# One tensor for keys and values, swapped slots, and six loads in place of nine for the last values

## The chip, the cores and the metric

The kernel runs on one core of one Trainium2 chip. The metric is the device time of one execution in microseconds (us); lower is better. The kernel before takes 1301.44 us (median of three runs, 1301.37 to 1301.44).

## The reference, cut to what matters

One decode step for two sequences (B = 2), width 448, 16 heads of 256, a cache of 8192 keys and values for each head and sequence, in float32. After the attention comes a gated bilinear feed-forward part of width 1792.

```python
q = (layernorm(x) @ wq)                       # 2 x 1 x 448 -> 16 heads x 256
scores = einsum("bhqd,bhkd->bhqk", q, k_cache) * 256 ** -0.5
p = softmax(scores)
o = einsum("bhqk,bhkd->bhqd", p, v_cache)
h = x + o.reshape(2, 1, 4096) @ wo
n = layernorm(h)
out = h + ((n @ w_gate) * (n @ w_up)) @ w_down
```

There are 32 pairs of head and sequence, called queries 0 to 31 here. Each reads 8 MiB of keys and 8 MiB of values once; with the weights that is 561 MB.

## The kernel before, in words

**Rows and loads.** A query's 8192 keys lie on 128 partitions, 64 keys on each, and one key has 256 floats. So a key tile or a value tile is 64 "rows" of 1 KB in every partition, and one row over all partitions is 128 KB of traffic. `k_sb` has 112 rows: two slots of 64 that share 16 rows (`k_base`, `OVER`). Even queries use rows 0 to 63, odd ones 48 to 111. `v_sb` has 64 rows. Nearly all loads are issued by SyncE (SP) on one queue, in program order; an issue waits until the rows that it overwrites are free, and all issues behind it wait too.

**One query.** VectorE (DVE) multiplies the keys by the query in place (`tensor_mul`) and sums over the 256 floats (`tensor_reduce`), in two parts: first the 16 rows that the next query's slot shares, then the other 48 (`score_parts`). `top` takes the maximum, `softmax` makes the weights p on ScalarE (ACT) with two small products on TensorE (PE), `mix` multiplies p with the values on PE in 64 matmuls of 512 columns, two rows of values for every two of them, and `mixed` turns the result and multiplies it with wo.

**Order of loads.** The loop at line 612 issues, in step n, the values of query n-1, then the keys of query n+1. PE runs the steps of the first `LOOP` queries in a hardware loop (`turns`). For the last queries (`LATE`, lines 25 to 30) the values come in several loads, so that rows freed early are filled early: query 28 in 48 and 16 rows, 29 in 32 and 32, 30 in 32 and 32 (the second into the rows of query 30's own keys), 31 in 16, 32 and 16. With a second part, step n loads the first part, then the keys n+1, then the second part. The keys of queries 30 and 31 (`FINE`) are scored in four parts of 16 rows.

**The end.** After query 31's scores come its softmax and `mix`; `open_sums` copies the residual sum out of PSUM (two DVE copies) and starts two sums with 16 small matmuls; it stands between the second and the third part of query 31's values. Then `last_head` (wo of head 15), the layer norm, `project` with w_gate, `project` twice with w_up, and `down` with w_down, whose tiles arrive in four loads (`DOWN`). The weights of this part are loaded into key rows as they come free. Small tiles of the end live in free value rows (`guest`, `late_guest`).

Of the kernel before, what the change touches and what calls it, by code (L numbers as in the profile page):

```python
# [7 lines left out]
ALU = mybir.AluOpType  # L8
AX = mybir.AxisListType
# [3 lines left out]
P = 128  # L13
# [5 lines left out]
OVER = HC  # L19

AHEAD = 24
FIRST = ((NJ - AHEAD, NJ), (0, NJ - AHEAD))


LATE = (
    ((48, None), (16, None)),
    ((32, None), (32, None)),
    ((32, None), (32, ("k", 0))),
    ((16, ("k", 32)), (32, ("v", 32)), (16, ("v", 0))),
)  # L30
WQ, WO = 3 * 2 * DH + DH, 2 * D
WALL = 2 * WQ + 4 * WO
# [183 lines left out]
def decode_block(nc, x, k_cache, v_cache, w, wg, wu, wd, out):  # L216
# [3 lines left out]
    def sb(name, *shape):  # L220
        return nc.alloc_sbuf_tensor(name, list(shape), F32)[:]
# [20 lines left out]
        put("PE", "transpose", out, in_, ident[:n, :n], r=(*r, "ident"), w=w, mark=mark)  # L242

    sb("align", P, ALIGN)
    k_sb = sb("k_sb", P, 2 * NJ - OVER, DH)
    v_sb = sb("v_sb", P, NJ, DH)
    w_sb = sb("w_sb", P, WALL)
    buffers = {"k": k_sb, "v": v_sb}
    v_flat = v_sb.rearrange("p j d -> p (j d)")

    def guest(name, at, rows, *shape):

        n = 1
        for k in shape:
            n *= k
        o.homes[name] = ("v", at, n)
        got = v_flat[:rows, at : at + n]
        if len(shape) > 1:
            dims = "abc"[: len(shape)]
            got = got.rearrange(f"p ({' '.join(dims)}) -> p {' '.join(dims)}", **dict(zip(dims, shape)))  # L260
        return got
# [5 lines left out]
        h, b = divmod(i, B)  # L267
        return cache[b, h].rearrange("(p j) d -> p j d", p=P)[:, lo:hi, :]

    def load_keys(name, cache, i, lo, hi, buf, at, event=None):  # L270
        o.load(
            "SP", name, buffers[buf][:, at : at + hi - lo, :], keys(cache, i, lo, hi),
            writes=[(buf, at * DH, (at + hi - lo) * DH)], event=event,
        )

    def k_base(i):
        return i % 2 * (NJ - OVER)

    def load_k(i, lo=0, hi=NJ):
        load_keys(f"d_k_{i}_{lo}", k_cache, i, lo, hi, "k", k_base(i) + lo)  # L280

    def v_parts(i):
        got, lo = [], 0
        for n, place in LATE[i - EARLY] if i >= EARLY else ((NJ, None),):
            buf, at = place or ("v", lo)
            got.append((lo, lo + n, buf, at))
            lo += n
        return got

    def load_v(i, part):  # L290
        lo, hi, buf, at = part
        load_keys(f"d_v_{i}_{lo}", v_cache, i, lo, hi, buf, at, "e_v" if i < LOOP else None)

    def load_w(name, k, lo, hi, event=None):
        o.load("SP", name, w_sb[:, lo:hi], w[k][:, lo:hi], writes=[("w", lo, hi)], event=event)
# [5 lines left out]
        return 2 * WQ + h % 4 * WO  # L301

    load_w("d_w0", 0, 0, WQ)
    for lo, hi in FIRST:
        load_k(0, lo, hi)

    ident = sb("ident", P, P)
    put("POOL", "memset", ident, 0.0, w=["ident"])
# [134 lines left out]
    def score_parts(i):  # L443
        if i == 0:
            return list(FIRST)
        at = [(k - 1) % (NJ // HC) * HC if i % 2 == 0 else k * HC for k in range(NJ // HC)]
        if i in FINE:
            return [(lo, lo + HC) for lo in at]
        return [(at[0], at[0] + HC), (at[1], at[1] + NJ - HC)]

    def scores(i, part, between=None):
        h, b = divmod(i, B)
        s, name = s_t[i % 2], f"s{i % 2}"
        lo, hi = score_parts(i)[part]
        at = k_base(i) + lo
        kt = k_sb[:, at : at + hi - lo, :]
        qk, there = kt, ("k", at * DH, (at + hi - lo) * DH)
        if i == 0 and part == 0:
            qk, there = v_sb[:, : hi - lo, :], ("v", 0, (hi - lo) * DH)
        q, slot = qs[b], q_at(h)  # L460
        here = ("k", at * DH, (at + hi - lo) * DH)
        dve(
            "tensor_mul", qk, kt, q[:, slot, :][:, None, :].to_broadcast([P, hi - lo, DH]),
            r=[here, (f"q{b}", slot, slot + 1)], w=[there],
        )
        if between is not None:
            between()
        dve("tensor_reduce", s[:, lo:hi], qk, axis=AX.X, op=ALU.add, r=[there], w=[(name, lo, hi)])

    def top(i):  # L470
        dve("tensor_reduce", m, s_t[i % 2], axis=AX.X, op=ALU.max, r=[f"s{i % 2}"], w=["m"],
# [24 lines left out]
    def mix(i, parts):  # L496
        k = other(i)
        with common(i):
            take("e_v", i, 16)
            for lo, hi, buf, at in parts:  # L500
                for t in range(lo // 2, hi // 2):
                    g, j = 32 * (t % 4), at + 2 * t - lo
                    mm(
                        o_ps[k][g : g + 2, :], p_t[k][:, 2 * t : 2 * t + 2],
                        buffers[buf][:, j : j + 2, :], t < 4, t >= NJ // 2 - 4,
                        r=[f"p{k}", (buf, j * DH, (j + 2) * DH)], w=[f"o_ps{k}"],
                        mark="PE" if t == hi // 2 - 1 else None,
                    )

# [71 lines left out]
    def group(t, q):  # L581
        return t[:, q * YW : (q + 1) * YW]

    late_at = [HC * DH]

    def late_guest(name, rows, *shape):
        got = guest(name, late_at[0], rows, *shape)
        late_at[0] += o.homes[name][2]
        assert late_at[0] <= 2 * HC * DH
        return got  # L590

    h_sb = late_guest("h_sb", B, DC * P)
# [19 lines left out]
    for n in range(NQ + 1):  # L612
        hp, at = divmod(n, 2 * B)
        parts = v_parts(n - 1) if n > 0 else []
        if n > 0:
            load_v(n - 1, parts[0])
        if n < NQ:
            scores(n, 0, (lambda: softmax(n - 1)) if n > 0 else None)
        else:
            softmax(n - 1)  # L620
        if late is not None:
            mix(n - 2, late)
            mixed(n - 2)
            late = None
        if n + 1 < NQ:
            load_k(n + 1)
        for part in parts[1:]:
            load_v(n - 1, part)
        if n % 8 == 1:
            k = n // 8 + 1  # L630
            load_w(f"d_w_{k}", k, WQ if k == H // 4 else 0, WALL, event("e_w", n))
        def norm_last():
            if n > 0:
                norm(n - 1)

        if n == NQ:
            norm_last()
        else:
            for part in range(1, len(score_parts(n))):
                scores(n, part, norm_last if part == 1 else None)  # L640
        if n == NQ:
            mix(n - 1, parts[:-1])
            open_sums()
            mix(n - 1, parts[-1:])
            mixed(n - 1)
        elif n + 1 < NQ and len(parts) > 1:
            late = parts[1:]
            mix(n - 1, parts[:1])
        elif n > 0:
            mix(n - 1, parts)  # L650
            mixed(n - 1)
        if at == 2 and hp + 1 < H // 2:
            queries(n - 1, hp + 1)
        if n < NQ:
            if n == 0:
                o.ops["PE"].append(lambda: turns())
            top(n)

    k_flat = k_sb.rearrange("p j d -> p (j d)")
    places = {"wd": 0, "wg": (NJ - OVER) * DH, "wu": (NJ - OVER) * DH + NF * D}  # L660
    wd_t, wg_t, wu_t = (k_flat[:, places[n] :][:, : NF * D] for n in ("wd", "wg", "wu"))
    for name, t, src in (("wg", wg_t, wg), ("wu", wu_t, wu)):
        for k, half in enumerate(PIECES[name]):
            o.load("SP", f"d_{name}_{k}", t[:, half], src[:, half],
                   writes=[("k", places[name] + half.start, places[name] + half.stop)])
    at = 0
    for n in DOWN:
        o.load("SP", f"d_wd_{at}", wd_t[:, at * D : (at + n) * D], wd[:, at * D : (at + n) * D],
               writes=[("k", at * D, (at + n) * D)])
        at += n  # L670

    o.load(
# [6 lines left out]

    def project(out, out_name, t, name, k, between=None):  # L680
        wide, piece = WIDE[{"wg": "B_w_gate", "wu": "B_w_up"}[name]][k], PIECES[name][k]
        here = ("k", places[name] + piece.start, places[name] + piece.stop)
        t = t[:, piece]
        for c in range(DC):
            for g in range(4):
                xs = xr[:, c]
                if c < DC - 1:
                    at = c * sum(wide) + sum(wide[:g])
                else:
                    xs = xr[:, c + g % 2]  # L690
                    at = 3 * sum(wide) + (wide[0] if g >= 2 else 0)
                mm(
                    out[32 * g : 32 * g + 32, : wide[g]], xs.rearrange("p b r -> p (b r)"),
                    t[:, at : at + wide[g]], c == 0, c == DC - 1, r=["xr", here], w=[out_name],
                    mark="PE" if c == DC - 1 and g == 3 else None,
                )
            if c == 1 and between is not None:
                between()
# [54 lines left out]
    def down(lo, hi):  # L753
        for k in range(lo, hi):
            n, g = FF[k]
            for q in range(YN):
                mm(
                    y_ps[32 * q : 32 * q + 32, :], hmT[n // 2][:, n % 2, g, :],
                    wd_t[:, k * D + q * YW : k * D + (q + 1) * YW], False, k == NF - 1,
                    r=[f"hmT{n // 2}", ("k", k * D, (k + 1) * D)], w=["y_ps"],  # L760
                    mark="PE" if k == NF - 1 and q == YN - 1 else None,
                )

# [94 lines left out]
```

## Time and profile before

| | |
|---|---|
| Median of three runs | 1301.44 us (1301.37 to 1301.44) |
| Profiled execution, span from first to last instruction | 1300.5 us |
| Around the span (median less span) | 0.9 us |
| DMA queue of SyncE, share of 16 engines' span | 99.8% (561.3 MB) |
| DVE busy | 1130.8 us (87%) |
| PE busy | 488.8 us (38%) |
| ACT busy | 62.6 us (5%) |
| TensorE clock granted, mean | 0.654 |

An engine's busy time is a mean over the whole span. Here one query follows the other with the same pattern for some 1150 us, and the last 150 us, in which the loads of the last queries and of the feed-forward weights and the final products run, are another stage with its own limits.

### The profile page before, as it was taken

The numbers are of one execution on the slowest core, as the hardware profiler recorded it, in microseconds if no ns is written. First come the engines' busy times: TensorE is split into PE (matmuls) and PEld (weight loads), VectorE is DVE, ScalarE is ACT, GpSimd is POOL, SyncE is SP. The second block draws the span as 40 slices with busy tenths as digits, with TensorE's granted clock in tenths as the row PEclk, the third lists the DMA queues.
The fourth block names the chain that finished last, engine by engine and source line by source line (L and its number), as shares of the span: only waits on it lengthen the run. The fifth ranks groups of instructions, "written<-read, shape, count | busy, mean of one in ns | idle before, by whom it ended". The sixth has DMA issues, their size and how long they took to land.

```text
span 1300.5 us, 6955 instructions
## 1 busy us (share of the span) xinstructions
PE 488.8 (38%) x2972; PEld 168.9 (13%) x2972; DVE 1130.8 (87%) x275; ACT 62.6 (5%) x184; POOL 1.4 (0%) x9
## 2 busy tenths in 40 slices
PE   3035422363331633215343063432424334243368
PEld 2011100120100201002101021010111001010113
DVE  7996988888988689888889868898888897889991
ACT  1000000000000000000000000000000000000000
POOL 0000000000000000000000000000000000000000
PEclk8566756686656766558666576665766667666578
DMA  9999999999999999999999999999999999999998
GB/s 414 423 434 448 424 437 431 427 441 423 448 424 435 448 423 443 427 439 429 435 435 423 433 448 423 448 424 443 427 443 427 423 436 445 426 438 429 435 433 374
DMA packets 12111, 561.45 MB, mean 432 GB/s; under 512 B 1602, under 2 KB 1732, under 8 KB 1988
## 3 DMA queue, kind: packets, MB, share of 16 engines
q1 hardware_dynamic: 12096, 561.30, 99.8%
q8 instruction: 6, 0.10, 0.0%
q14 instruction: 5, 0.04, 0.0%
q10 hardware_dynamic: 4, 0.00, 0.0%
HBM read 561.19 MB, written 0.11 MB: 432 GB/s over the span
## 4 chain that ended last, share of the span: by engine, by line
DMA 70%; DVE 29%; PE 0%; issue 0%; SPq 0%
DMA k_sb<-in_A_k_cache_dram 68%; DVE k_sb L229 14%; DVE s L229 14%; DMA k_sb<-in_wd_dram 2%; DVE nm L229 0%; PE y_ps L229 0%; SPq L176 0%; DVE m L229 0%; PE sm L229 0%; DVE v_sb L229 0%; DVE rl L229 0%
## 5 line engine op out<-in xcount | busy, mean ns | idle before, releaser
L229 DVE TENSOR_TENSOR k_sb<-k_sb,q 128x12288 f32<-128x12288 f32 (+2 forms) x67 | 549.6, 8203 | 130.3 <-DMA k_sb<-in_A_k_cache_dram 130.3
L229 DVE TENSOR_REDUCE s<-k_sb 128x48 f32<-128x12288 f32 (+2 forms) x67 | 549.3, 8198 | 0.2
L229 PE MATMUL o_ps<-v_sb,p 128*2 128x512 f32 x2000 | 288.2, 739 | 397.7 <-PEq L183 387.6
L229 PEld LDWEIGHTS o_ps<-v_sb,p 128*2 128x2 f32 x2000 | 53.7, 97 | 603.8 <-issue 591.3
L229 PE MATMUL sm<-nm,ones 1*128 1x1 f32 x64 | 16.6, 326 | 191.7 <-PEq L183 175.1
L229 PE MATMUL sm<-ident,m 128*1 128x128 f32 x32 | 10.9, 341 | 137.0 <-PEq L183 106.1
L229 PE MATMUL q_ps<-w_sb,xb 128*128 128x256 f32 (+1 forms) x172 | 59.3, 503 | 0.0
L229 ACT ACTIVATE o_sb<-o_ps 128x512 f32<-128x512 f32 x32 | 19.1, 597 | 703.9 <-PE o_ps L229 703.9
L229 PE MATMUL sm<-sel,o_sb 128*128 128x1 f32 x256 | 33.7, 253 | 25.8 <-PEq L183 22.9
L229 PE MATMUL acc_ps<-w_sb,oT 128*2 128x448 f32 x60 | 36.6, 749 | 15.9 <-PEq L183 11.0
L229 PEld LDWEIGHTS sm<-nm,ones 1*128 1x128 f32 x64 | 14.6, 283 | 201.2 <-issue 183.5
L229 PEld LDWEIGHTS sm<-sel,o_sb 128*128 128x128 f32 x256 | 31.8, 195 | 55.6 <-issue 48.2
L229 PEld LDWEIGHTS q_ps<-w_sb,xb 128*128 128x128 f32 x172 | 33.7, 200 | 30.0 <-issue 27.6
L229 PE MATMUL sm<-lsum,ones 128*128 128x1 f32 x64 | 17.5, 342 | 26.0 <-PEq L183 23.1
L229 ACT ACTIVATE nb<-sm 128x1 f32<-128x1 f32 x32 | 5.5, 171 | 395.7 <-PE sm L229 395.7
L229 PEld LDWEIGHTS sm<-ident,m 128*1 128x1 f32 x32 | 2.6, 81 | 149.8 <-issue 115.3
L229 PEld LDWEIGHTS sm<-lsum,ones 128*128 128x128 f32 x64 | 15.6, 303 | 28.0 <-issue 24.7
L229 ACT ACTIVATE q<-q_ps,rstd 128x512 f32<-128x512 f32 (+1 forms) x18 | 11.5, 640 | 71.9 <-PE q_ps L229 71.9
L229 PE MATMUL o_ps<-k_sb,p 128*2 128x512 f32 x48 | 9.3, 934 | 6.1 <-DMA k_sb<-in_A_v_cache_dram 6.1
L229 ACT ACTIVATE p<-s,nb 128x64 f32<-128x64 f32 x32 | 11.1, 347 | 1.0
L229 DVE TENSOR_TENSOR v_sb<-k_sb,q 128x6144 f32<-128x6144 f32 x1 | 6.6, 6557 | 4.8 <-DMA k_sb<-in_A_k_cache_dram 4.8
L229 PE MATMUL q_ps<-k_sb,xr 128*32 128x256 f32 (+3 forms) x96 | 10.0, 506 | 1.6 <-DMA k_sb<-in_B_w_gate_dram 1.6
(79 smaller groups left out, 85.1 us busy)
## 6 DMA issues: line engine op xcount, KB each, us to landing
v_sb<-in_A_v_cache_dram SPq DMA_DIRECT2D x4, 4096.0 KB, 30.5
w_sb<-in_w_dram SPq DMA_DIRECT2D x3, 3584.0 KB, 37.8
v_sb<-in_A_v_cache_dram SPq DMA_DIRECT2D x1, 6144.0 KB, 24.3
k_sb<-in_A_k_cache_dram SPq DMA_DIRECT2D x1, 5120.0 KB, 24.6
v_sb<-in_A_v_cache_dram SPq DMA_DIRECT2D x2, 2048.0 KB, 27.3
k_sb<-in_A_v_cache_dram SPq DMA_DIRECT2D x1, 4096.0 KB, 35.3
k_sb<-in_B_w_gate_dram SPq DMA_DIRECT2D x1, 3136.0 KB, 32.4
k_sb<-in_A_k_cache_dram SPq DMA_DIRECT2D x1, 3072.0 KB, 11.6
```

The source lines that it names most:

```text
L229: o.put(engine, lambda: f(*args, **kw), r, w, mark, event)
```

## The change

- Keys and values share one tensor `c_sb` of 176 rows: rows 0 to 111 for keys as before, rows 112 (`RING`) to 175 for values. The total size is unchanged.
- The key slots are swapped: even queries use rows 48 to 111, odd ones 0 to 63. The first 24 keys of query 0 go to the value rows and are multiplied in place there; before, 24 keys were loaded to their key rows and their product was written to the value rows.
- `LATE` has three entries, so query 28's values are one load of 64 rows and belong to the hardware loop. Query 29's come in 32 and 32 rows, query 30's in one load of 64 rows to rows 64 to 127 (48 key rows and 16 value rows), query 31's in 44 rows (rows 128 to 171) and 20 rows (rows 64 to 83).
- The product of query 30's first 16 keys is written to rows 160 to 175, not in place.
- `open_sums` stands before all of query 31's `mix`.
- The feed-forward weights' places: w_gate from row 0, w_up from row 24.5, w_down from row 84.

```diff
-FIRST = ((NJ - AHEAD, NJ), (0, NJ - AHEAD))
+FIRST = ((0, AHEAD), (AHEAD, NJ))
+RING = 2 * NJ - OVER
 LATE = (
-    ((48, None), (16, None)),
-    ((32, None), (32, None)),
-    ((32, None), (32, ("k", 0))),
-    ((16, ("k", 32)), (32, ("v", 32)), (16, ("v", 0))),
+    ((32, RING), (32, RING + 32)),
+    ((64, NJ),),
+    ((44, RING + HC), (20, NJ)),
 )
...
     def k_base(i):
-        return i % 2 * (NJ - OVER)
+        return (1 - i % 2) * (NJ - OVER)
...
-        at = [(k - 1) % (NJ // HC) * HC if i % 2 == 0 else k * HC for k in range(NJ // HC)]
+        at = [(k - i % 2) % (NJ // HC) * HC for k in range(NJ // HC)]
...
-        at = k_base(i) + lo
-        kt = k_sb[:, at : at + hi - lo, :]
-        qk, there = kt, ("k", at * DH, (at + hi - lo) * DH)
-        if i == 0 and part == 0:
-            qk, there = v_sb[:, : hi - lo, :], ("v", 0, (hi - lo) * DH)
+        at = RING if i == 0 and part == 0 else k_base(i) + lo
+        to = RING + NJ - HC if i == NQ - 2 and part == 0 else at
+        k_t, t = (c_sb[:, r : r + hi - lo, :] for r in (at, to))
+        here, there = rows(at, hi - lo), rows(to, hi - lo)
...
         if n == NQ:
-            mix(n - 1, parts[:-1])
             open_sums()
-            mix(n - 1, parts[-1:])
+            mix(n - 1, parts)
             mixed(n - 1)
...
-    places = {"wd": 0, "wg": (NJ - OVER) * DH, "wu": (NJ - OVER) * DH + NF * D}
+    places = {"wg": 0, "wu": NF * D, "wd": (NJ + 20) * DH}
```

## Rows read from the trace of the kernel before

**Rows 1.** The page: span, throughput by slice, the load queue's share.
```profile
span 1300.5 us, 6955 instructions
...
GB/s 414 423 434 448 424 437 431 427 441 423 448 424 435 448 423 443 427 439 429 435 435 423 433 448 423 448 424 443 427 443 427 423 436 445 426 438 429 435 433 374
...
q1 hardware_dynamic: 12096, 561.30, 99.8%
```

**Rows 2.** Timeline of DVE: start, duration, tiles; idle before and its releaser.
```profile
1159.42 4.43 DVE L229 TENSOR_TENSOR k_sb<-k_sb,q 128x4096 f32<-128x4096 f32 x1 [3.58 <-DMA k_sb<-in_A_k_cache_dram]
...
1194.38 4.42 DVE L229 TENSOR_TENSOR k_sb<-k_sb,q 128x4096 f32<-128x4096 f32 x1
...
1198.91 4.40 DVE L229 TENSOR_REDUCE s<-k_sb 128x16 f32<-128x4096 f32 x1
...
1225.25 4.42 DVE L229 TENSOR_REDUCE s<-k_sb 128x16 f32<-128x4096 f32 x1
...
1260.71 4.42 DVE L229 TENSOR_REDUCE s<-k_sb 128x16 f32<-128x4096 f32 x1
...
1268.20 0.72 DVE L229 COPY v_sb<-acc_ps 2x448 f32<-2x448 f32 x2
...
1281.57 0.57 DVE L229 COPY xr<-sm 128x96 f32<-128x96 f32 x3 [0.74 <-PE sm L229]
```

**Rows 3.** Timeline of SyncE's issues in the last 135 us.
```profile
1168.39 0.33 SPq L176 DMA_DIRECT2D k_sb<-in_A_k_cache_dram  x1
1168.76 13.36 SPq L176 DMA_DIRECT2D v_sb<-in_A_v_cache_dram  x2
1203.34 0.33 SPq L176 DMA_DIRECT2D k_sb<-in_A_k_cache_dram  x1
1204.53 9.87 SPq L176 DMA_DIRECT2D v_sb<-in_A_v_cache_dram  x2
...
1298.87 0.34 SPq L176 DMA_DIRECT2D out_dram<-v_sb  x1
```

**Rows 4.** DMA issues between 1160 and 1170 us: size, us from issue to landing.
```profile
v_sb<-in_A_v_cache_dram SPq DMA_DIRECT2D x1, 2048.0 KB, 29.3
k_sb<-in_A_k_cache_dram SPq DMA_DIRECT2D x1, 24.8
```

**Rows 5.** DMA issues: one between 1204 and 1206 us, two from the page.
```profile
v_sb<-in_A_v_cache_dram SPq DMA_DIRECT2D x1, 4096.0 KB, 32.4
...
k_sb<-in_A_v_cache_dram SPq DMA_DIRECT2D x1, 4096.0 KB, 35.3
...
out_dram<-v_sb SPq DMA_DIRECT2D x1, 56.0 KB, 1.6
```

**Rows 6.** Timeline of PE's matmuls in the last 45 us.
```profile
1256.26 5.87 PE L229 MATMUL o_ps<-k_sb,p 128*2 128x512 f32 x32 [6.05 <-DMA k_sb<-in_A_v_cache_dram]
...
1268.01 3.40 PE L229 MATMUL o_ps<-k_sb,p 128*2 128x512 f32 x16
1271.23 3.61 PE L229 MATMUL o_ps<-v_sb,p 128*2 128x512 f32 x32
1274.77 0.40 PE L229 MATMUL o_ps<-v_sb,ident 2*2 2x128 f32 x8
1274.99 0.37 PE L229 MATMUL y_ps<-v_sb,pair 2*32 2x112 f32 x8
1275.63 1.90 PE L229 MATMUL o_ps<-v_sb,p 128*2 128x512 f32 x16 [0.27 <-DMA v_sb<-in_A_v_cache_dram]
...
1283.13 3.63 PE L229 MATMUL q_ps<-k_sb,xr 128*32 128x512 f32 x16 [1.60 <-DMA k_sb<-in_B_w_gate_dram]
...
1295.17 0.59 PE L229 MATMUL y_ps<-k_sb,v_sb 128*32 128x112 f32 x16
1296.47 2.03 PE L229 MATMUL y_ps<-k_sb,v_sb 128*32 128x112 f32 x64 [0.71 <-DMA k_sb<-in_wd_dram]
```

**Rows 7.** Windows: busy us of PE, PEld, DVE, ACT, POOL; PE clock; DMA share; GB/s.
```profile
1268.00:1271.00 3.00, 3.00 (x17) 0.47 (x20) 1.21 (x6) 0.00 (x0) 0.00 (x0) 0.50 0.83 350
1271.00:1274.00 3.00, 3.00 (x32) 0.70 (x32) 0.00 (x0) 0.00 (x0) 0.00 (x0) 0.99 1.07 457
...
1283.00:1287.00 4.00, 3.87 (x18) 1.33 (x18) 0.29 (x2) 0.00 (x0) 0.00 (x0) 0.50 1.01 431
```

More of the change, by code (lines that the diff above doesn't have):

```diff
@@ L244, in decode_block @@
     sb("align", P, ALIGN)
-    k_sb = sb("k_sb", P, 2 * NJ - OVER, DH)
-    v_sb = sb("v_sb", P, NJ, DH)
+    c_sb = sb("c_sb", P, RING + NJ, DH)
+    v_sb = c_sb[:, RING:, :]
     w_sb = sb("w_sb", P, WALL)
-    buffers = {"k": k_sb, "v": v_sb}
-    v_flat = v_sb.rearrange("p j d -> p (j d)")
+    c_flat = c_sb.rearrange("p j d -> p (j d)")
     def guest(name, at, rows, *shape):
@@ L255, in guest @@
             n *= k
-        o.homes[name] = ("v", at, n)
-        got = v_flat[:rows, at : at + n]
+        at += RING * DH
+        o.homes[name] = ("c", at, n)
+        got = c_flat[:rows, at : at + n]
         if len(shape) > 1:
@@ L268, in keys, with rows, load_keys @@
         return cache[b, h].rearrange("(p j) d -> p j d", p=P)[:, lo:hi, :]
-    def load_keys(name, cache, i, lo, hi, buf, at, event=None):
+    def rows(at, n):
+        return ("c", at * DH, (at + n) * DH)
+    def load_keys(name, cache, i, lo, hi, at, event=None):
         o.load(
-            "SP", name, buffers[buf][:, at : at + hi - lo, :], keys(cache, i, lo, hi),
-            writes=[(buf, at * DH, (at + hi - lo) * DH)], event=event,
+            "SP", name, c_sb[:, at : at + hi - lo, :], keys(cache, i, lo, hi),
+            writes=[rows(at, hi - lo)], event=event,
         )
     def k_base(i):
-        return i % 2 * (NJ - OVER)
+        return (1 - i % 2) * (NJ - OVER)
     def load_k(i, lo=0, hi=NJ):
-        load_keys(f"d_k_{i}_{lo}", k_cache, i, lo, hi, "k", k_base(i) + lo)
+        load_keys(f"d_k_{i}_{lo}", k_cache, i, lo, hi, k_base(i) + lo)
     def v_parts(i):
         got, lo = [], 0
-        for n, place in LATE[i - EARLY] if i >= EARLY else ((NJ, None),):
-            buf, at = place or ("v", lo)
-            got.append((lo, lo + n, buf, at))
+        for n, at in LATE[i - EARLY] if i >= EARLY else ((NJ, RING),):
+            got.append((lo, lo + n, at))
             lo += n
@@ L290, in load_v @@
     def load_v(i, part):
-        lo, hi, buf, at = part
-        load_keys(f"d_v_{i}_{lo}", v_cache, i, lo, hi, buf, at, "e_v" if i < LOOP else None)
+        lo, hi, at = part
+        load_keys(f"d_v_{i}_{lo}", v_cache, i, lo, hi, at, "e_v" if i < LOOP else None)
     def load_w(name, k, lo, hi, event=None):
@@ L303, in decode_block @@
     load_w("d_w0", 0, 0, WQ)
-    for lo, hi in FIRST:
-        load_k(0, lo, hi)
+    load_keys("d_k_first", k_cache, 0, *FIRST[0], RING)
+    load_k(0, *FIRST[1])
     ident = sb("ident", P, P)
@@ L454, in scores @@
         lo, hi = score_parts(i)[part]
-        at = k_base(i) + lo
-        kt = k_sb[:, at : at + hi - lo, :]
-        qk, there = kt, ("k", at * DH, (at + hi - lo) * DH)
-        if i == 0 and part == 0:
-            qk, there = v_sb[:, : hi - lo, :], ("v", 0, (hi - lo) * DH)
+        at = RING if i == 0 and part == 0 else k_base(i) + lo
+        to = RING + NJ - HC if i == NQ - 2 and part == 0 else at
+        k_t, t = (c_sb[:, r : r + hi - lo, :] for r in (at, to))
+        here, there = rows(at, hi - lo), rows(to, hi - lo)
         q, slot = qs[b], q_at(h)
-        here = ("k", at * DH, (at + hi - lo) * DH)
         dve(
-            "tensor_mul", qk, kt, q[:, slot, :][:, None, :].to_broadcast([P, hi - lo, DH]),
+            "tensor_mul", t, k_t, q[:, slot, :][:, None, :].to_broadcast([P, hi - lo, DH]),
             r=[here, (f"q{b}", slot, slot + 1)], w=[there],
@@ L467, in scores @@
             between()
-        dve("tensor_reduce", s[:, lo:hi], qk, axis=AX.X, op=ALU.add, r=[there], w=[(name, lo, hi)])
+        dve("tensor_reduce", s[:, lo:hi], t, axis=AX.X, op=ALU.add, r=[there], w=[(name, lo, hi)])
     def top(i):
@@ L499, in mix @@
             take("e_v", i, 16)
-            for lo, hi, buf, at in parts:
+            for lo, hi, at in parts:
                 for t in range(lo // 2, hi // 2):
@@ L504, in mix @@
                         o_ps[k][g : g + 2, :], p_t[k][:, 2 * t : 2 * t + 2],
-                        buffers[buf][:, j : j + 2, :], t < 4, t >= NJ // 2 - 4,
-                        r=[f"p{k}", (buf, j * DH, (j + 2) * DH)], w=[f"o_ps{k}"],
+                        c_sb[:, j : j + 2, :], t < 4, t >= NJ // 2 - 4,
+                        r=[f"p{k}", rows(j, 2)], w=[f"o_ps{k}"],
                         mark="PE" if t == hi // 2 - 1 else None,
@@ L582, in group @@
         return t[:, q * YW : (q + 1) * YW]
-    late_at = [HC * DH]
+    late_at = [0]
     def late_guest(name, rows, *shape):
@@ L588, in late_guest @@
         late_at[0] += o.homes[name][2]
-        assert late_at[0] <= 2 * HC * DH
+        assert late_at[0] <= HC * DH
         return got
@@ L657, in decode_block @@
             top(n)
-    k_flat = k_sb.rearrange("p j d -> p (j d)")
-    places = {"wd": 0, "wg": (NJ - OVER) * DH, "wu": (NJ - OVER) * DH + NF * D}
-    wd_t, wg_t, wu_t = (k_flat[:, places[n] :][:, : NF * D] for n in ("wd", "wg", "wu"))
+    places = {"wg": 0, "wu": NF * D, "wd": (NJ + 20) * DH}
+    wd_t, wg_t, wu_t = (c_flat[:, places[n] :][:, : NF * D] for n in ("wd", "wg", "wu"))
     for name, t, src in (("wg", wg_t, wg), ("wu", wu_t, wu)):
@@ L664, in decode_block @@
             o.load("SP", f"d_{name}_{k}", t[:, half], src[:, half],
-                   writes=[("k", places[name] + half.start, places[name] + half.stop)])
+                   writes=[("c", places[name] + half.start, places[name] + half.stop)])
     at = 0
@@ L668, in decode_block @@
         o.load("SP", f"d_wd_{at}", wd_t[:, at * D : (at + n) * D], wd[:, at * D : (at + n) * D],
-               writes=[("k", at * D, (at + n) * D)])
+               writes=[("c", places["wd"] + at * D, places["wd"] + (at + n) * D)])
         at += n
@@ L681, in project @@
         wide, piece = WIDE[{"wg": "B_w_gate", "wu": "B_w_up"}[name]][k], PIECES[name][k]
-        here = ("k", places[name] + piece.start, places[name] + piece.stop)
+        here = ("c", places[name] + piece.start, places[name] + piece.stop)
         t = t[:, piece]
@@ L759, in down @@
                     wd_t[:, k * D + q * YW : k * D + (q + 1) * YW], False, k == NF - 1,
-                    r=[f"hmT{n // 2}", ("k", k * D, (k + 1) * D)], w=["y_ps"],
+                    r=[f"hmT{n // 2}", ("c", places["wd"] + k * D, places["wd"] + (k + 1) * D)],
+                    w=["y_ps"],
                     mark="PE" if k == NF - 1 and q == YN - 1 else None,
```

## The prediction

> **What bounds the kernel now.** I read the page first, its throughput line and load queue above all. The queue's packets fill 99.8% of the 16 engines' span, and the slices hold between 414 and 448 GB/s until the last, whose 374 contains the final calculation [rows 1]. So the kernel is bound by its 561 MB of traffic, and no rearrangement of loads can bring more than the little that is left around the stream. Second I read DVE's timeline: up to query 29 DVE waits some 3.6 us for each query's keys (the wait of 3.58 us ahead of 1159.42 is the last), and from there it works without a pause until query 31's last score at 1265.13 (1260.71 plus 4.42) [rows 2]. Third, SyncE's issues and the landing times, which tell how much of the queue is still to come when an issue happens [rows 3 to 5]. Last, PE's timeline of the end [rows 6]. There the reader is to see two small slacks: PE waits for w_gate until 1283.13, although its other operand is ready at 1282.14 (1281.57 plus 0.57) [rows 2, 6], so 1.0 us; and it waits 0.71 us for w_down ahead of the last 64 matmuls [rows 6]. The time of 1301.44 us is thus set by the last bytes of w_down, for which PE waits until 1296.47, with a chain of calculation that is 1.0 us early at one place and 0.7 us at another. The sum below is made against the span of 1300.5 us; the median of the runs is 0.9 us above it, and I carry that 0.9 over. A change of 0.2% is 2.6 us; smaller ones can hardly be told from none here.
>
> **The change, part by part.**
>
> *One tensor, swapped slots, first keys, places of the weights.* Bytes, instruction shapes and the size of the tensor stay, and so does the rule that neighbouring queries share 16 rows. The first 24 keys of query 0 are still multiplied by one instruction of the same size. The keys of query 1 can be issued at once, not after that product, but the queue is full at that time anyway [rows 1], so this is hidden behind the bytes ahead of it. Cost: 0. If that cover were missing, it would be a gain of the gap, of which the slices show none.
>
> *Six loads for nine.* What could be saved is a fixed cost of each load. The 2048 KB load (16 rows) that follows the keys of query 30 lands at 1198.1 (1168.76 plus 29.3), 4.9 us after the keys at 1193.2 (1168.39 plus 24.8) [rows 3, 4]. That is 428 GB/s for a small load between large ones, within the slices' 414 to 448. At 434, 2.1 MB need 4.83 us, so a fixed cost is some 0.1 us and three loads less bring 0 to 0.3 us. I take 0.
>
> *Query 28's values as one load.* This is the step that costs. Before, 48 rows are issued, then the keys of query 30, then 16 rows. After, all 64 rows stand ahead of the keys. The queue works in order, so those keys land 4.9 us later, at 1198.1 in place of 1193.2 [rows 4]. DVE takes them up at 1194.38 before, at once behind the scores of query 29 [rows 2]; that hid 1.2 us. After, it waits until 1198.1, which is 3.7 us of delay. From there on DVE has no slack to the end (1194.38 to 1265.13 without a pause), so query 31's last score ends at 1268.85.
>
> *The product in other rows.* Its size stays (4.42 us). It frees the shared rows when the product ends, not when its sum ends. So the keys of query 31 can be issued at about 1202.5 (1198.1 plus 4.4), where by the old rule it would be 1207.0, with the stream ahead of them ending at about 1207.7: the queue holds 5 us more. Queued behind this issue on SyncE are query 29's second part and all later loads. It hides the delay from the queue; it gives DVE nothing.
>
> *Query 30's values in one load.* They go to rows of query 30's own keys 16 to 63 and must wait for all its scores: 1229.67 before (1225.25 plus 4.42) [rows 2], 1233.4 after. The load ahead lands at 1236.9 (1204.53 plus 32.4) [rows 3, 5], so 3.5 us of queue are left. A small store needs 1.6 us from issue to landing [rows 5], which bounds the start of a load from above; no gap, but only 2 us from one. Its landing stays at about 1256.2 (the 1256.26 start of PE) [rows 6]. PE then has 64 matmuls, not 32: the 32 took 5.87 us and 32 more at the full clock take 3.61 [rows 6], so about 9.4 and the end at 1265.7. The last 20 rows of query 31 wait for that, and behind them on SyncE are w_gate, w_up and w_down. The 44 rows ahead (5.77 MB at 434 GB/s) land 13.3 us after 1256.2, at 1269.5; 3.8 us are left. All at the low clock the 64 matmuls would take 13.6 us (four times 3.40) and a gap of 2 us would open; all at the full one 7.2. The sum takes no gap.
>
> *`open_sums` first, then all of query 31's values.* Before, PE starts these values at 1268.01, when the softmax's last product ends, and the two copies on DVE (1268.20 to 1268.92) and the 16 small matmuls (0.6 us) run beside and between [rows 2, 6]. After, PE stands in order behind them: copies, then 16 matmuls, at half the clock some 1.2 us, so the start is 2.2 us later. Together with DVE's 3.7 it is 1273.9. By then the rest has landed or lands in time (the last at about 1275.6, as before [rows 6]). 64 matmuls as in the rows, 16 at the low clock and 48 at the full one, take 3.40 + 3.61 + 1.90 = 8.9 us; bounds 7.2 and 13.6. End 1282.8, where it was 1277.53: 5.3 later.
>
> *The rest of the chain.* From that end to the operand of `project` it was 4.6 us (1277.53 to 1282.14), after 1287.4; w_gate has long landed, so 1.0 of the 5.3 us goes into PE's old wait: the start is 4.3 later than 1283.13. From there to the end of the matmuls ahead of the wait for w_down it was 12.63 us (1283.13 to 1295.76), after 1300.1, and the last 64 then run without waiting: 1.8 us (2.03 less about 0.2 of waiting for the last piece). End of PE 1301.9 against 1298.50: +3.4 us, if PE meets the clock as before.
>
> It need not. Before, `project` began with the granted clock at 0.50, the 1.2 GHz level, and the second half ran mostly at 2.4 [rows 6, 7]: the first 16 matmuls took 3.63 us, where at the full clock half of that. The stretch ahead of it is as sparse as before, so PE will again fall to the low level, but when it falls and rises relative to `project` shifts with the 4.3 us. Fully at 2.4 GHz the chain is 2.3 us shorter (+1.1); with the low level lasting somewhat longer there or in query 31's values (32 matmuls, not 16, at half speed: 1.5 us) it is +4.9. I take half of the 2.3 off: +2.2 us, span 1302.7, time 1303.6. Here the clock is a term of the sum, since the end is now PE's and no longer the last byte's.
>
> The Trainium skill ("TensorE: Matmul & The Clock Gate", Part 1: the HAM clock gate) says that the throttled level is the default and that activity releases it. The trace agrees: 0.50 at 1268 to 1271 behind a pause, 0.99 right after [rows 7]. By its default level throughout, `project` would stay slow and the result would be at the upper bound.
>
> **The rivals.**
>
> *A: the low clock lasts as long as before or longer* (0.38). Same steps, +2.7 to +5 us: 1304.1 to 1306.4, slower by more than 0.2%. For it: the stretch of small products ahead of `project` is the same, and it was at 0.50 for all of 1283 to 1287 [rows 7]. Against it: PE comes from a longer dense run of 64 matmuls. It decides where low-clock work in the two dense runs exceeds that of before by nothing: +2.6 us is reached with some 1.6 us of the 2.3 lost.
>
> *B: the queue runs dry* (0.05) at query 30's values or query 31's last 20 rows. If the first is issued 3 us later than I work out, or its matmuls stay at the low clock, the last byte lands 2 to 4 us later; up to 2 us is hidden behind PE's lateness. 1304 to 1307, slower.
>
> *C: the delay is hidden* (0.07): the keys come early enough, or PE runs at the full clock in both dense runs (8.9 to 7.2 and 2.3 less). 1301.2 to 1302.3, no change. For it: 1.0 and 0.7 us of slack; against it: 5.3 us are to be covered.
>
> *D: each load has a fixed price that is now saved* (0.03). With the store's 1.6 us [rows 5] for each of three loads: 4.8 us, 1296.6, faster. Against it: the 428 GB/s of the small load between its neighbours, and 99.8% of queue [rows 1, 4]. The Trainium skill ("DMA: Bandwidth & Descriptors", Anatomy of one DMA) gives 2.0 us fixed for a transfer of the GpSimd path and advises large batches; by it three loads would be 6 us, 1295.4. The trace does not bear it out for queued loads.
>
> **How the numbers follow.** My forecast, 1302.4 to 1304.0 with 1303.6 as its time, has 0.47: the lateness of DVE and PE is real, the clock gives some of it back, and it stays within 0.2%. With C this makes 0.54 for no change; A and B make 0.43 for slower; D 0.03 for faster. The range from 1301.5 to 1305.8 holds the forecast, the larger part of A and half of C.
>
> **What would show it.** Right: DVE waits some 3.7 us for query 30's keys, behind 1194.3; query 31's last score ends near 1268.9; PE starts its values near 1274 and ends them near 1283; `project` has no wait for w_gate; no wait for w_down is left ahead of the last 64 matmuls, and the last load lands near 1298 as before. Wrong: no wait for query 30's keys; a DMA share below 1 between 1233 and 1275; or a stretch from `project` to the end far from the 10 to 15 us that I allow.

## The result and the profile after

The changed kernel takes 1303.79 us, the median of 16 runs (1302.66 to 1305.18), against 1301.45 us for the kernel before (16 runs, 1301.31 to 1301.82). The ratio is 1.0019, with a 95% interval from 1.0012 to 1.0026: slower by 0.19%, 2.3 us. The forecast was 1303.6.

The runs of the changed kernel fall into two groups, eight from 1302.66 to 1303.52 and seven from 1304.90 to 1305.18, with one at 1304.06; those of the kernel before stay within 0.5 us. The execution with the profile is of the upper group: it took 1304.95 us with a span of 1303.6.

The page of the changed kernel, its span and the share of the load queue:

```profile
span 1303.6 us, 6968 instructions
...
q1 hardware_dynamic: 11664, 561.30, 99.6%
```

The bytes are the same and the queue is nearly as full. The span around it is longer: the last load of w_down now lands 5.1 us before the span ends (at 1298.49 of 1303.6), where it was 2.4 us (1298.06 of 1300.5).

The timeline of DVE in the changed kernel (start, duration, tiles, idle time before and what ended it), the lines that answer to [rows 2]:

```profile
1159.09 4.43 DVE L229 TENSOR_TENSOR c_sb<-c_sb,q 128x4096 f32<-128x4096 f32 x1 [3.60 <-DMA c_sb<-in_A_k_cache_dram]
...
1197.78 4.42 DVE L229 TENSOR_TENSOR c_sb<-c_sb,q 128x4096 f32<-128x4096 f32 x1 [3.65 <-DMA c_sb<-in_A_k_cache_dram]
...
1228.66 4.42 DVE L229 TENSOR_REDUCE s<-c_sb 128x16 f32<-128x4096 f32 x1
...
1264.12 4.42 DVE L229 TENSOR_REDUCE s<-c_sb 128x16 f32<-128x4096 f32 x1
...
1271.62 0.72 DVE L229 COPY c_sb<-acc_ps 2x448 f32<-2x448 f32 x2
...
1287.51 0.57 DVE L229 COPY xr<-sm 128x96 f32<-128x96 f32 x3 [1.12 <-PE sm L229]
```

The reader is to see a second wait for keys, 3.65 us ahead of 1197.78, where the kernel before had none, and no wait from there on: query 31's last score ends at 1268.54 (1264.12 plus 4.42), 3.4 us later than before. As this execution runs 0.33 us ahead at query 29 (1159.09 against 1159.42), the delay is 3.7 us.

SyncE's issues in the changed kernel, against [rows 3]:

```profile
1168.05 0.33 SPq L176 DMA_DIRECT2D c_sb<-in_A_k_cache_dram  x1
1187.88 0.33 SPq L176 DMA_DIRECT2D c_sb<-in_A_v_cache_dram  x1
1202.23 0.33 SPq L176 DMA_DIRECT2D c_sb<-in_A_k_cache_dram  x1
...
1266.11 0.43 SPq L176 DMA_DIRECT2D c_sb<-in_B_w_gate_dram  x1
...
1302.04 0.34 SPq L176 DMA_DIRECT2D out_dram<-c_sb  x1
```

The keys of query 30 are issued when they were before, at 1168.05; all that changed is what stands ahead of them. The keys of query 31 follow at 1202.23, as soon as the product ends.

PE's matmuls of the end in the changed kernel, against [rows 6]:

```profile
1255.73 9.93 PE L229 MATMUL o_ps<-c_sb,p 128*2 128x512 f32 x64 [4.81 <-DMA c_sb<-in_A_v_cache_dram]
...
1270.91 0.58 PE L229 MATMUL sm<-lsum,ones 128*128 128x1 f32 x2 [0.73 <-ACT p L229]
1272.39 0.60 PE L229 MATMUL o_ps<-c_sb,ident 2*2 2x128 f32 x8 [0.90 <-DVE c_sb L229]
1272.77 0.60 PE L229 MATMUL y_ps<-c_sb,pair 2*32 2x112 f32 x8
1273.30 9.68 PE L229 MATMUL o_ps<-c_sb,p 128*2 128x512 f32 x64
...
1288.14 3.63 PE L229 MATMUL q_ps<-c_sb,xr 128*32 128x512 f32 x16 [0.67 <-DVE xr L229]
...
1299.54 2.12 PE L229 MATMUL y_ps<-c_sb 128*32 128x112 f32 x80
```

Query 31's values start at 1273.30 and end at 1282.98, where they ended at 1277.53. `project` no longer waits for w_gate but for its own operand `xr`, and the 80 matmuls of `down` run in one piece with no wait for w_down. So the end has passed from the load queue to PE.

Windows of the changed kernel (the three numbers at the end are the PE clock, the DMA share and GB/s):

```profile
1273.00:1278.00 5.00, 5.00 (x32) 0.85 (x28) 0.00 (x0) 0.00 (x0) 0.00 (x0) 0.50 0.99 424
1278.00:1283.00 5.00, 4.98 (x44) 0.91 (x36) 0.00 (x0) 0.00 (x0) 0.00 (x0) 0.93 0.99 427
...
1288.00:1292.00 4.00, 3.86 (x18) 1.24 (x18) 1.07 (x7) 0.00 (x0) 0.00 (x0) 0.50 1.01 430
```

A PE clock of 0.50 is the lower level, 1.2 GHz. In this execution the first half of query 31's values and the first half of `project` run at it.

### The profile page after: what moved, and what is told of

Read it like the earlier page. It is cut to its first block, busy times and chain, and to the rows that moved or that the text cites. A ratio compares the mean times of both kernels' runs of the same rounds, so it can differ in the third digit from the quotient of the medians.

```text
span 1303.6 us, 6968 instructions
## 1 busy us (share of the span) xinstructions
PE 483.1 (37%) x2972; PEld 169.4 (13%) x2972; DVE 1131.1 (87%) x275; ACT 62.6 (5%) x184; POOL 1.4 (0%) x9
## 3 DMA queue, kind: packets, MB, share of 16 engines
q1 hardware_dynamic: 11664, 561.30, 99.6%
## 5 line engine op out<-in xcount | busy, mean ns | idle before, releaser
L229 DVE TENSOR_TENSOR c_sb<-c_sb,q 128x4096 f32<-128x4096 f32 (+1 forms) x68 | 556.1, 8178 | 137.5 <-DMA c_sb<-in_A_k_cache_dram 137.3
L229 DVE TENSOR_REDUCE s<-c_sb 128x16 f32<-128x4096 f32 (+1 forms) x68 | 555.8, 8174 | 0.2
L229 PE MATMUL o_ps<-c_sb,p 128*2 128x512 f32 x2048 | 295.0, 740 | 406.7 <-PEq L183 398.9
L229 PEld LDWEIGHTS o_ps<-c_sb,p 128*2 128x2 f32 x2048 | 55.3, 97 | 620.2 <-issue 610.6
L229 PE MATMUL acc_ps<-w_sb,oT 128*2 128x448 f32 x60 | 32.4, 672 | 15.8 <-PEq L183 11.0
L229 ACT ACTIVATE oT<-sm,rl 128x2 f32<-128x2 f32 x32 | 8.4, 262 | 38.4 <-PE sm L229 38.4
L229 PE MATMUL q_ps<-c_sb,xr 128*32 128x256 f32 (+3 forms) x96 | 9.5, 487 | 0.7 <-DVE xr L229 0.7
## 6 DMA issues: line engine op xcount, KB each, us to landing
c_sb<-in_A_k_cache_dram SPq DMA_DIRECT2D x1, 3072.0 KB, 11.4
```

What stands on the lines that cost most here:

```text
L229: o.put(engine, lambda: f(*args, **kw), r, w, mark, event)
```

## The experiments

The theory is that of the prediction: DVE's lateness of 3.7 us, PE's later start behind `open_sums`, and the clock. Rival 1 puts the cost on the clock alone, rival 2 on the load queue. Each kernel's runs stand beside runs of the kernel before on the same chip (medians 1301.41 to 1301.45).

### 1. The keys of query 30 early again

```diff
 LATE = (
+    ((48, RING), (16, RING + 48)),
     ((32, RING), (32, RING + 32)),
...
-        to = RING + NJ - HC if i == NQ - 2 and part == 0 else at
+        to = at
```

> The changed kernel with query 28's values again in 48 and 16 rows around the keys of query 30, and with the product of query 30's first 16 keys in place. Theory (the keys of query 30 come 4.9 us later, DVE and all of the end move by 3.7 us): the keys land near 1193, DVE does not wait for them, query 31's last score ends near 1265.0 (1268.5 in the changed kernel), PE starts query 31's values near 1269.8 and ends them near 1278 to 1279.5; time 1301.4 to 1302.2. Rival 1 (PE's clock and its one block of 64 matmuls cost the time, not DVE's lateness): DVE is early, but the end stays, 1303 to 1305. Rival 2 (the load queue of the changed kernel moves bytes less well or runs dry; more and smaller loads help or hurt): the last w_down load lands at another time than 1298.5 by more than 1 us.

1301.65 us (11 runs, 1301.20 to 1302.62), ratio 1.0001 [0.9992, 1.0010]. DVE in this kernel has no wait at query 30, and PE starts query 31's values 3.65 us earlier than in the changed kernel:

```profile
1193.93 4.42 DVE L230 TENSOR_TENSOR c_sb<-c_sb,q 128x4096 f32<-128x4096 f32 x1
...
1260.27 4.42 DVE L230 TENSOR_REDUCE s<-c_sb 128x16 f32<-128x4096 f32 x1
```

```profile
1269.65 9.94 PE L230 MATMUL o_ps<-c_sb,p 128*2 128x512 f32 x64
...
1296.22 2.12 PE L230 MATMUL y_ps<-c_sb 128*32 128x112 f32 x80
```

All but 0.2 us of the loss is gone with this step, though the block of 64 matmuls takes as long as in the changed kernel (9.94 us), the first 16 of `project` do too (3.63 us), and `open_sums` still stands in front. The other line of the edit, the product in place, makes nothing faster by itself (run 3). Rival 1 falls as the cause. So does rival 2: large loads, one tensor and swapped slots are still in. The last load of w_down lands 1.0 us earlier than in the changed kernel (1297.50 against 1298.49), which only just misses that rival's sign; but in the changed kernel PE works for 3.2 us behind that landing (until 1301.66), so it did not set the end there.

### 2. `open_sums` between the values

```diff
+            mix(n - 1, parts[:-1])
             open_sums()
-            mix(n - 1, parts)
+            mix(n - 1, parts[-1:])
```

> The changed kernel with open_sums between query 31's 44 and 20 rows of values. Theory (open_sums in front holds PE's values up by 1.8 us, from 1271.5 to 1273.3): PE starts them at 1271.5 and spends 0.6 us on the sums later, so the end comes 0.5 to 1.5 us earlier, 1302.4 to 1303.3 as a median, the low-clock cases included. Rival 1 (clock alone): no change beyond the scatter, 1303.8. Rival 2 (stream): 1303.8.

1304.10 us (11 runs, 1303.29 to 1305.69), 0.3 us above the changed kernel's first 16 runs: no gain, a miss. Since the two groups of the changed kernel lie 2 us apart, a second pair was run later on one chip, first the changed kernel as it is:

> The changed kernel as it is, beside the next run on one chip. Every theory: 1302.7 to 1305.2, median 1303.3 to 1304.5; it is the measure for the next run.

1305.27 us (7 runs, 1304.89 to 1305.48), all of the upper group. And the edit again:

> The changed kernel with open_sums between query 31's 44 and 20 rows, a second time. Theory as it was (the position costs 1 to 2 us of PE's start and so of the end): median 0.5 to 1.5 us below the run beside it. Rival (what PE gains by starting earlier it gives back by working longer at the low clock, so the position is no matter): within 0.4 us of the run beside it.

1303.61 us (11 runs, 1302.70 to 1305.04), 1.7 us below the run beside it. Taken together, the changed kernel's 23 runs have a median of 1304.9 and the edit's 22 one of 1304.0. The pair on one chip has the theory's direction, the first comparison has not; whether the position costs anything here, and how much up to 1.7 us, is not settled, because the scatter of either kernel is larger than the difference.

### 3. The product in place

```diff
-        to = RING + NJ - HC if i == NQ - 2 and part == 0 else at
+        to = at
```

> The changed kernel with the product of query 30's first 16 keys in place. Theory: the keys of query 31 are issued at 1206.7, not at 1202.2, when 0.7 us or less of the queue are left; the queue has a gap of 0.5 to 2 us, all later loads land that much later (w_down near 1299 to 1300.5 in place of 1298.5), but the end is PE's, so the time stays within 0.5 us of the changed kernel's, 1303.3 to 1304.3. Rival 2 (the stream sets the end): 0.5 to 2 us slower, 1304.3 to 1305.8. Rival 1 (clock alone): as the theory.

1304.84 us (9 runs, 1304.38 to 1305.42), ratio 1.0025 [1.0015, 1.0035]. The windows of this kernel around the issue of query 31's keys, which is at 1207.18 here:

```profile
1206.00:1207.00 1.00, 0.00 (x0) 0.00 (x0) 1.00 (x1) 0.00 (x0) 0.00 (x0) 0.50 0.15 66
1207.00:1208.00 1.00, 0.11 (x4) 0.11 (x8) 1.00 (x2) 0.00 (x0) 0.00 (x0) 0.50 0.00 0
1208.00:1209.00 1.00, 1.00 (x8) 0.15 (x4) 1.00 (x1) 0.00 (x0) 0.00 (x0) 0.50 2.97 1049
```

The gap is there: between 1207 and 1208 no packet of the queue begins. (A window counts a packet where it starts, so the one after shows more than 1.) And PE now waits for w_down at the end, in the same kernel:

```profile
1300.09 2.04 PE L229 MATMUL y_ps<-c_sb 128*32 128x112 f32 x64 [0.72 <-DMA c_sb<-in_wd_dram]
```

The wait for the second load of w_down ends at 1300.09; in the kernel before it ended at 1296.47, and in the changed kernel this load lands at 1296.87. So the queue is 3.2 us later than in the changed kernel, and it sets the end again. Of the 3.2 us, 2.3 are there when the keys of query 31 land (1228.98 against 1226.70), and 0.4 were there before the gap (DVE takes up query 30's keys at 1198.21, not 1197.78). So the gap itself is some 1.9 us, as expected; where the last 0.9 us are lost no run shows. All nine runs lie above the changed kernel's lower group, near or in its upper one, so in time this kernel cannot be told from that group. The mechanism is as expected, and the part about the end is rival 2's. So moving the product is what keeps the queue full once query 28's values are one load.

### 4. PE kept busy

```diff
+    def warm(n):
+        for k in range(n):
+            g = 32 * (k % 4)
+            mm(q_ps[1][g : g + 2, :], ident[:, :2], w_sb[:, :512], True, True,
+               r=["ident", ("w", 0, 512)], w=["q_ps1"], mark="PE")
```

`warm(1)` to `warm(3)` stand in eight of PE's pauses between the end of query 30's `mixed` and `project`. Together they make 16 products (the expectation counts 17; the trace has 32 matmuls of them, two for each).

> The changed kernel with 17 extra small products in PE's pauses from query 31's softmax to the first project, into a PSUM bank that is free then; they add work and change no result. Theory (some 1 to 3 us of the end are low clock in query 31's values and in project): the granted clock is at the full level from query 31's values or soon after and in project, the scatter shrinks below 1.5 us, the median falls to 1301.6 to 1302.8. Rival (lateness alone, the clock is no term): 1303.5 to 1304.3 with the same scatter of 2.5 us.

1302.57 us (11 runs, 1302.14 to 1303.34), ratio 1.0008 [0.9999, 1.0017]. The windows and PE's timeline of this kernel:

```profile
1273.00:1278.00 5.00, 5.00 (x52) 1.24 (x52) 0.00 (x0) 0.00 (x0) 0.00 (x0) 1.00 1.02 436
...
1283.00:1288.00 5.00, 5.00 (x44) 2.16 (x40) 2.28 (x13) 0.28 (x1) 0.00 (x0) 1.00 0.97 415
```

```profile
1272.98 7.05 PE L229 MATMUL o_ps<-c_sb,p 128*2 128x512 f32 x64
...
1297.59 2.11 PE L229 MATMUL y_ps<-c_sb 128*32 128x112 f32 x64 [0.69 <-DMA c_sb<-in_wd_dram]
```

At the full clock the 64 matmuls take 7.05 us, not 9.68, and PE is early enough to wait for w_down again. The scatter shrinks from 2.5 to 1.2 us. So the clock is a term: 1.2 us of the median by the first 16 runs, more against the upper group. It cannot give more, as the last bytes take over. They come later here than in the kernel before: the wait for the second load of w_down ends at 1297.59, not at 1296.47, and that 1.1 us is what this kernel's median still lies above the kernel before on the same chip (1302.57 against 1301.42). Why the queue is later is not shown: it has no gap like that of run 3, as the keys of query 31 land as early as in the changed kernel (1226.62 against 1226.70).

The same with `open_sums` between the values, to read its price at the full clock:

> The changed kernel with the 17 extra small products in PE's pauses and open_sums between query 31's 44 and 20 rows. At the full clock the position can be read from the profile by itself: theory, PE starts the values some 1 us earlier than with open_sums in front (there 1272.98, last score at 1268.46) and ends them 0.4 to 1 us earlier (there 1279.9); the time is 1302.0 to 1302.6, since the last bytes of w_down set most of it. Rival (the position costs nothing even at the full clock): the values end at the same distance from the last score, 11.4 us.

1302.68 us (11 runs, 1302.31 to 1304.17). In its profile the extra products themselves met the low clock (two of them took 1.86 us, where two took 1.02 in the run before) and ran into PE's work, and the values ended 14.0 us behind the last score, not 11.4 or less. Inconclusive for the price of the position.

### 5. The kernel before with one load for query 28

```diff
-    ((48, None), (16, None)),
+    ((64, None),),
```

> The kernel before with one edit: query 28's values in one load of 64 rows (all else as before, the product in place). Theory: the keys of query 30 land 4.9 us later, DVE waits 3.7 us, query 31's last score ends near 1268.8; the keys of query 31 are issued near 1207.1 with under 1 us of queue left, so the queue runs dry as in the run with the product in place and the last w_down load lands 2 to 3 us later than before, near 1300 to 1301; both give 1303.5 to 1305. Rival 1 (DVE's lateness is not what costs, the changed end is): 1301.4 to 1302. Rival 2 (the lateness of PE alone, no gap in the queue): 1302 to 1303.4, w_down landing near 1298.

1304.44 us (11 runs, 1304.24 to 1304.96), ratio 1.0023 [1.0014, 1.0032]. DVE's wait for the keys of query 30 is there, and PE starts query 31's values 3.3 us later than in the kernel before:

```profile
1197.70 4.42 DVE L229 TENSOR_TENSOR k_sb<-k_sb,q 128x4096 f32<-128x4096 f32 x1 [3.58 <-DMA k_sb<-in_A_k_cache_dram]
```

```profile
1271.35 3.59 PE L229 MATMUL o_ps<-k_sb,p 128*2 128x512 f32 x16
...
1298.58 2.40 PE L229 MATMUL y_ps<-k_sb,v_sb 128*32 128x112 f32 x80
```

One line of the change, put alone into the kernel before, costs 3.0 us. The run does not single out DVE's lateness, though. The product is in place here, so the queue has a gap like that of run 3 as well (the keys of query 31 land at 1229.59, in the kernel before at 1227.09), and the last load of w_down lands 2.5 us later than in the kernel before (1300.54 against 1298.06). PE ends 0.44 us behind that landing in both kernels, so the last bytes set this end too. But the 80 matmuls take 2.40 us, where they take 2.12 without a wait, so PE's late chain would have ended only some 0.3 us sooner by itself.

### 6. The kernel before with `open_sums` first

> The kernel before with one edit: open_sums ahead of all of query 31's values. Theory: PE starts them 1.6 to 2.2 us later, near 1269.7, and ends them 0.5 to 2 us later, near 1278 to 1279.5; the 1.7 us of slack ahead of project and of the last matmuls take most of it, 1301.4 to 1302.1. Rival (each us that PE starts later shows at the end): 1303 to 1303.6.

1301.43 us (11 runs, 1301.28 to 1301.89), ratio 1.0000 [0.9991, 1.0009]. PE starts the values at 1269.53, some 1.9 us later for an execution that is 0.4 ahead, and still waits for w_down at the end:

```profile
1269.53 3.60 PE L229 MATMUL o_ps<-k_sb,p 128*2 128x512 f32 x16
...
1296.12 2.02 PE L229 MATMUL y_ps<-k_sb,v_sb 128*32 128x112 f32 x64 [0.71 <-DMA k_sb<-in_wd_dram]
```

Where the queue sets the end, the position costs nothing.

### 7. Both undone, and PE kept busy with early keys

> The changed kernel with query 28's values in 48 and 16 rows, the product in place, and open_sums between query 31's 44 and 20 rows: undone are DVE's lateness and the late start of PE, kept are the swapped slots, one tensor, query 30's single load and 44 and 20 rows. Theory: the end is set by the last bytes of w_down again, 1301.2 to 1301.7, with less scatter than with open_sums in front (1301.2 to 1302.6 there). Rival (the position of open_sums is no matter, as the run with it between suggested): the same scatter, median 1301.6.

1301.71 us (11 runs, 1301.33 to 1303.14): the median as expected, the scatter not.

> The changed kernel with query 28's values in 48 and 16 rows, the product in place, and the 17 extra small products in PE's pauses. Theory: PE is early and at the full clock, the last bytes of w_down set the end in every execution: 1300.9 to 1301.5, scatter under 0.5 us, not clearly better than before, because the bytes are the floor. Rival (PE still sets the end in the run without the extra products): 0.3 us or more faster than 1301.4, clear of it.

1301.88 us (11 runs, 1301.24 to 1303.37): a miss, some 0.4 us more than expected and no smaller scatter. DVE's line in the first of these kernels shows why PE is late there without any lateness of the keys:

```profile
1264.97 0.22 DVE L230 TENSOR_REDUCE m<-s 128x1 f32<-128x64 f32 x1
1267.90 0.28 DVE L230 TENSOR_REDUCE nm<-sm 1x1 f32<-1x128 f32 x1 [2.71 <-PE sm L230]
```

The maximum of query 31 waits 2.71 us for PE, whose 64 matmuls for query 30's single load (10.02 us from 1255.94 in this profile) stand in front of it; in the kernel before 32 were left at that time and the wait was 0.47 us:

```profile
1265.85 0.28 DVE L229 TENSOR_REDUCE nm<-sm 1x1 f32<-1x128 f32 x1 [0.47 <-PE sm L229]
```

In the second kernel the extra products stand there as well, and the wait is 2.78. So query 30's one load has a price of its own on PE, which the changed kernel hides behind DVE's lateness. It is not all of the scatter: in the first kernel's profile (1302.48 us) the last load of w_down lands 0.7 us later than in the kernel before (1298.76 against 1298.06), with PE ending 0.44 us behind it again, and why it is later is not shown. None of these kernels beats the kernel before: the last bytes are the floor.

### 8. One more profile of the changed kernel

> The changed kernel as it is, one more profile, to see the clock in one of its faster executions (1302.7 to 1303.5) if it is one. Theory: in such an execution the low clock takes 3 us or more less of the stretch from query 31's values to the end of project than in the slower ones (there 1268.4 to 1278.7 and 1285.5 to 1292.3). Rival: the same low stretches in both groups, and the difference lies elsewhere, in the landing of the loads for one.

1305.65 us, so not one of the faster executions, but it shows another cause of scatter. PE's end, SyncE's last issue and the DMA rows from 1300 us to the end, in this execution:

```profile
1298.42 2.12 PE L229 MATMUL y_ps<-c_sb 128*32 128x112 f32 x80
```

```profile
1300.91 0.34 SPq L176 DMA_DIRECT2D out_dram<-c_sb  x1
```

```profile
q8 instruction: 1, 0.02, 1.8%
...
out_dram<-c_sb SPq DMA_DIRECT2D x1, 56.0 KB, 3.4
```

PE is 1.1 us earlier than in the first profile, and yet the execution is 0.7 us longer, because the final store takes 3.4 us and not 1.6. In that time one packet of instructions (16 KB, 1.8% of 16 engines over the 5 us from 1300, so some 1.4 us of one engine) is on a DMA engine too. In the first profile of the changed kernel and in that of the kernel before, no instruction packet falls behind 1300 or 1297 us, and the store takes 1.6. That the packet held up the store is what the rows suggest; no run took it away.

PE's dense stretches in this execution are the two lines below; in the first profile they took 9.68 and 3.63 us:

```profile
1273.61 9.11 PE L229 MATMUL o_ps<-c_sb,p 128*2 128x512 f32 x64
...
1287.36 2.99 PE L229 MATMUL q_ps<-c_sb,xr 128*32 128x512 f32 x16 [0.66 <-DVE xr L229]
```

The granted clock is 1.00 from 1283 to 1288 and 0.57 from 1288 to 1292, where the first profile has 0.75 and 0.50. PE is 1.1 us earlier although query 31's last score ends 0.3 us later (1268.85). With a store of 1.6 us this execution would have taken some 1303.8, between the two groups. So more of the full clock does make the changed kernel faster, as the theory says. The mean clock listed with each run points the same way: 0.660 for the eight runs of the lower group, 0.654 for the seven of the upper. That is a mean over the whole run, and in the kernel before it varies from 0.649 to 0.665 without such groups; a profile of the lower group itself was not taken, so the cause of the two groups stays likely, not shown.

## Why the prediction was right

*Query 28's values as one load*: worked out 3.7 us of waiting, measured 3.65 and the last score 3.7 us late by its own execution. Run 1 shows that it is the cause: with the keys early the loss is gone. Run 5 shows that this one line costs 3.0 us in the kernel before, but there the lateness and the gap in the queue come together.

*The product in other rows*: right that it keeps the queue from running dry and gives DVE nothing. Without it (run 3) the queue has a gap of some 1.9 us, is 3.2 us later at the end than in the changed kernel, and sets the time again. I had counted the reserve at the issue to the landing of the load ahead, 1207.85 in run 3 (1187.60 plus 20.3). But most of the queue's engines run out of packets earlier than that: hardly a packet begins from 1206 on, while the issue comes at 1207.18 and the first packets after 1208. The reserve has to be counted to the time when the engines run out of packets, and some 1 us from the issue to the first packet added. That the gaps at the two tight issues did not come up in the changed kernel (99.6% of a span that is 3 us longer) was right, by less margin than I thought.

*`open_sums` first*: PE's start was 2.2 us later by the sum and 1.8 by the trace (1271.49, the end of the softmax's last product, to 1273.30). Its share of the end is not shown: run 2 gives 0.3 us the wrong way in one comparison and 1.7 us in the other, and in run 6, where the queue sets the end, it is 0.

*The blocks of 64 and the rest of the chain*: query 30's block was worked out at 9.4 us and took 9.93, ending at 1265.66 where 1265.7 was expected. For query 31's values I had worked out 8.9 us and an end at 1282.8; measured are 9.68 and 1282.98. `project` was to start at 1287.4 and started at 1288.14; PE was to end at 1301.9 at the old clock and ended at 1301.66. That agreement is in part luck: the values took 0.8 us more than worked out, the stretch from them to `project` 5.2 us and not 4.6, and the stretch from there to the end 13.5 us and not 14.5. The waits for w_gate and for the last w_down loads are gone, as said, and the last load lands at 1298.5. Span against span, the profiled execution is 3.1 us longer, near the +3.4 for the unchanged clock.

*The clock*: half of 2.3 us was taken off for executions with more of the full clock; the median came out at +2.3 us where I had +2.2. Run 4 shows that the clock is worth 1.2 us of that median. The agreement to 0.2 us is better than the working: the second set of the changed kernel had 1305.27, in the range but on the side of rival A, and run 8 shows a store that was no term at all, as was the later landing of the last bytes that run 4 met. That rival had 0.38, and with 14 of 23 runs at 1304.9 or above it deserved at least as much as the forecast.

*Carried over*: I added 0.9 us around the span, from the median and a profile of another execution. Runs of the kernel before with both numbers give 1.3 (1301.52 us with a span of 1300.2), and the changed kernel's profiled run 1.35. The two errors cancel: the profiled execution of before was one of the longer ones, so the forecast was +2.2 us in span and in time alike.

## What to carry to other kernels

Where one queue is full from start to end, the order of its loads is the schedule: merging two loads that stood around a third delays the third by the bytes that now stand ahead of it (here 16 rows, 4.9 us of queue), and that counts if its reader has no slack from there on. A step that is hidden by 1 us of slack gives no gain when it is sped up and a loss when it is delayed, so read how much slack the last stages have before trading loads for simplicity. When the end passes from a queue to TensorE, the scatter can grow too: here from 0.5 to 2.5 us, and back to 1.2 us once PE's pauses were filled, so part of it is the clock that the dense blocks meet.

## What the runs showed of the hardware

With the queue all but empty, no packet began in the 0.8 us after an issue at 1207.18 (run 3), and packets of nearly 3 us on each of the 16 engines began in the next 1 us. A store of 56 KB that took 1.5 to 1.6 us in the other profiles took 3.4 us in run 8, where one instruction packet was on an engine at the same time; that the packet is the reason is not shown. Sixteen small products in PE's pauses held the granted clock at 1.00 from 1268 to 1292 (run 4), and the 64 matmuls took 7.05 us in place of 9.68; with the same products in run 4's second kernel the clock was 0.66 from 1268 to 1273, so they did not hold it every time.
